# A list scheduler that keeps the port shared by GpSimd and VectorE as a resource, with all sums of activations on VectorE

## The chip, the cores and the metric

The kernel runs on one core of one Trainium2 chip. The metric is the device time of one execution in microseconds, as the median of the runs of a kernel; a profile of one further execution stands beside it.

## The reference

Three blocks are computed, all in float32. The attention block has 2 batches of 8 heads, 576 positions, 64 wide: a local attention (|i-j| < 4) plus an attention over means of 4 positions, repeated back up. Its output becomes x for two mixtures of experts:

```python
# MoE 1: N, D, E, F = 1152, 512, 8, 1024
P = np.exp(logits - logits.max())          # logits = x @ w_gate
for _ in range(8):                         # "gate rounds" below
    P /= P.sum(1, keepdims=True) + 1e-09
    P /= P.sum(0, keepdims=True) + 1e-09
    P *= N / E
for e in range(E):
    out += P[:, e:e + 1] * (np.maximum(x @ w1[e], 0.0) @ w2[e])
# MoE 2: the same with 4 experts; its P is given with the inputs
```

## The kernel before

All values are split into two parts, hi (rounded for TensorE) and lo (the rest), and each product runs as three passes (hi hi, hi lo, lo hi). A value `xh`, `xl` is such a pair. The first products `x @ w1` are not done block by block: as in Strassen's scheme, 7 products of sums of blocks take the place of 8, and a second level of the same scheme lies inside ("deep" products, line L507). So two kinds of sums are needed. **Sums of weights** (L355, and their lo parts at L328) are made anew for every expert, all on GpSimd (POOL in the profile). **Sums of activations** are made once for MoE 1 and once for MoE 2: `x_sums(j)`, four calls for four quarters of the tokens, adds hi and lo back to a whole value (L1129), combines four of those (L1135, into `tmp`), stores the combination (DMA to `kept`, L1145), and splits it again into `sh` (ScalarE, L1147) and `sl` (VectorE, L1149); `deep_sums(p, ...)` does the same for the second level of product p (L1209 for all its two-operand steps, L1228 for the hi part on ScalarE, into `sx`).

Before, these activation sums are dealt out between POOL and VectorE (DVE in the profile): L1129 is always on POOL, the rest by two tables.

```python
ON_POOL = (3, 5, 6, 7)              # L411: deep_sums of these products on POOL
X_POOL0, X_POOL = (1, 3), (0, 2)    # L1397: x_sums of these quarters on POOL, MoE 1 and MoE 2
```

The hidden layer leaves PSUM at L424 (ScalarE, relu, hi part) and L426 (VectorE, lo part): `own<-bank` where the source is in PSUM (a bank), `own<-tmp` where it was brought to SBUF before, so that L426 has two operands in SBUF. L482 adds banks, L527 copies a bank into another as the start of a product ("seed"; the product L507 then adds to it), L674 is the second product, L709 to L719 add its result to the output. At the start of MoE 2, `turn` (L1251 to L1263) brings MoE 1's output back as `xh`, `xl`. The gate of MoE 1 makes logits (L1279, copied out at L1286), transposes them (L1335, L1359), and does its eight rounds: row sums on VectorE (L1321 to L1325), column sums as a product with ones on TensorE (L1383), and L1386 to L1392 on VectorE.

The order on every engine is written out by `Plan`: each task is added with an engine, a cost in ns, what it reads and writes; `run` then takes, step by step, the task that can begin first by these costs, among the first 48 of each engine, and emits it. Queues are in order on the chip, so this order stays. There are two plans: one for attention and the first weights (up to about 71 us), a second one for all that follows.

Of the kernel before, what the change touches and what calls it, by code (L numbers as in the profile page):

```python
# [94 lines left out]
class Plan:  # L95
# [5 lines left out]
    QUEUE = 1  # L101
    PULL = 0.0
    OVER = dict.fromkeys(AFTER, 0.0)

    def __init__(self):
        self.tasks, self.last, self.readers = [], {}, {}
        self.clock, self.later, self.bias = 0.0, [], 0.0
        self.ranks, self.step = (), None

    def add(self, eng, cost, fn, reads=(), writes=(), slack=0.0, after=()):  # L110
        n = len(self.tasks)
        if self.step is not None:
# [22 lines left out]
        deps.discard(n)  # L135
        if eng == "PE":
            self.clock += cost
        self.tasks.append((eng, cost, fn, sorted(deps), bufs, self.clock + slack + self.bias))
        while self.later and self.clock >= self.later[0][0]:
            self.later.pop(0)[1]()  # L140

    def run(self, free=None, idle=None):
# [29 lines left out]
        for _ in range(len(T)):  # L172
            best = None
            for e in engines:
                look = self.QUEUE if e == "DMA" else self.LOOK
                mine = None
                for i in todo[e][:look]:
                    t = start(i)
                    if t is None:
                        continue  # L180

                    v = t + self.PULL * T[i][5]
                    if mine is None or v < mine[0] - 1e-9:
                        mine = (v, t, i)
# [5 lines left out]
            t, i, e = best  # L190
            if e == "PE":
                stall += t - free[e]
            _, cost, fn, _, bufs, _ = T[i]
            for b in bufs:
                if b.slot is not None:
                    continue
                since = b.ring.free()[0] + 150.0
                b.ring.give(b)
                if e == "PE" and idle is not None:
                    idle(b, t - max(free[e], since))  # L200
            if e == "DMA":
# [16 lines left out]
def tile_attention_moe_moe(  # L218
# [191 lines left out]
    SUMS = (0, 5, 2), (4, 3)  # L410
    ON_POOL = (3, 5, 6, 7)  # L411

# [7 lines left out]
    def hidden(src, key, s, b, u, c0, slack=0.0):  # L420
# [6 lines left out]
            out=ht[:, s, 1, c:c + U], in0=src(), scalar=0.0, in1=ht[:, s, 0, c:c + U].bitcast(F32),  # L427
            op0=ALU.max, op1=ALU.subtract), (key, (*k, 0)), ((*k, 1),), slack=slack)

    P_EVICT, S_EVICT = (412.0, 457.0), (420.0, 900.0)  # L430

# [676 lines left out]
    extra = [late.tile([128, U], F32, name=f"sum_{j}") for j in range(3)]  # L1108
    SHARED, PARTS = 900.0, 860.0
    SHARED_X, PARTS_X = 900.0, 900.0  # L1110
    LAG = 18000.0
# [3 lines left out]
    def x_sums(j, on_pool=False):  # L1115
# [21 lines left out]

# [5 lines left out]
        for i, t in enumerate((a22, a11, a21, a12)):  # L1143
# [58 lines left out]
    def deep_sums(p, g, on_pool):  # L1202
# [117 lines left out]
    def gate_rows():  # L1320
# [5 lines left out]
            out=pv, in0=pv, in1=sm_["rs"].unsqueeze(2).to_broadcast([128, NN, E1]), op=ALU.mult),  # L1326
            ("rs",), ("p",))

    def gate_start():
# [12 lines left out]
        def fill_eps():  # L1342
# [36 lines left out]
    def gate_round(it):  # L1379
        pc = r_bank.new()  # L1380
        def fn():
# [12 lines left out]
            in1=sm_["cs"].unsqueeze(1).to_broadcast([128, NN, E1]), op0=ALU.mult, op1=ALU.mult),  # L1394
            ("cs",), ("p", *done))
# [215 lines left out]
```

## Time and profile before

| what | value |
|---|---|
| median of 3 runs | 1176.58 us (1174.29 to 1176.61) |
| profiled execution, its time | 1174.57 us |
| its span in the profile | 1172.8 us |
| TensorE busy | 1151.8 us, 98% |
| VectorE busy | 845.7 us, 72% |
| GpSimd busy | 965.5 us, 82% |

The span runs from the first to the last instruction; the time of the same execution is 1.8 us more. Shares of busy time are averages over a span of very different stages: attention up to about 66 us, the gate and the first products of MoE 1 up to about 200, a long even stretch to 790, the passage to MoE 2 up to about 910, and an even stretch again.

### The profile page before, as it was taken

What the parts mean: (1) busy time and instruction counts of PE and PEld (TensorE: products, weight loads), DVE (VectorE), ACT (ScalarE), POOL (GpSimd) and SP (SyncE); (2) the same over time, 40 slices, a digit from 0 to 9 for tenths busy, and PEclk for the clock granted to TensorE, in tenths of its full rate; (3) what the DMA queues carried; (4) which work ended last, traced back from release to release, by engine and by line L of the source; (5) the groups of instructions that cost most, each with busy time, mean ns of one, the idle gap of its engine ahead of it and who ended that gap; (6) DMA issues with size and microseconds to landing.
All of it is one profiled execution on the core that took longest, in us unless ns stands there. A gap on an engine that the chain in (4) does not pass through costs nothing.

```text
span 1172.8 us, 22043 instructions
## 1 busy us (share of the span) xinstructions
PE 1151.8 (98%) x7361; PEld 1026.2 (87%) x7361; DVE 845.7 (72%) x1803; ACT 668.4 (57%) x1679; POOL 965.5 (82%) x1081
## 2 busy tenths in 40 slices
PE   9989899999999999999999999999799999999998
PEld 7868888988988988988988988989698898898897
DVE  7869789677668668568568568578788776766764
ACT  5844546755655655656556556535475565565561
POOL 7979958898798798798798798739999979879870
PEclk9999899999999999999999999999899999999999
DMA  8525344544544544544554654632535555555544
GB/s 247 161 96 169 131 136 145 181 164 158 184 159 158 180 166 152 184 168 146 188 171 138 195 167 139 207 113 82 177 123 166 175 179 163 164 173 164 161 159 144
DMA packets 110946, 188.66 MB, mean 161 GB/s; under 512 B 13360, under 2 KB 26416, under 8 KB 110832
## 3 DMA queue, kind: packets, MB, share of 16 engines
q1 hardware_dynamic: 110832, 187.25, 50.0%
q8 instruction: 58, 0.95, 0.3%
q14 instruction: 56, 0.46, 0.1%
HBM read 128.22 MB, written 58.98 MB: 160 GB/s over the span
## 4 chain that ended last, share of the span: by engine, by line
PE 85%; POOL 7%; DMA 3%; DVE 2%; issue 2%; ACT 1%; SPq 0%; POOLq 0%; DVEq 0%; ACTq 0%
PE bank L674 46%; PE bank L507 33%; PE bank L467 2%; POOL tmp L1129 1%; POOL raw L355 1%; PE bank L306 1%; POOL w2s L328 1%; POOL tmp L1135 1%; DMA v<-in_v_dram 1%; POOL own L328 1%; DVE sl L1149 1%; POOL sx L1209 1%; PE bank L1010 1%; DVE sx L1209 1%; PE bank L850 1%
## 5 line engine op out<-in xcount | busy, mean ns | idle before, releaser
L674 PE MATMUL bank<-w2s,own 128*128 128x512 f32 (+1 forms) x2604 | 671.4, 392 | 0.0
L674 PEld LDWEIGHTS bank<-w2s,own 128*128 128x128 f32 x2604 | 462.0, 188 | 69.5
L482 DVE TENSOR_TENSOR bank<-bank,tmp 128x288 f32<-128x288 f32 x540 | 221.7, 458 | 139.8 <-PE bank L507 64.6
L328 POOL TENSOR_TENSOR own<-raw,own 128x512 fp32r<-128x512 f32 (+1 forms) x204 | 244.0, 1205 | 56.0 <-ACT own L326 55.2
L355 POOL TENSOR_TENSOR raw<-raw,raw 128x128 f32<-128x128 f32 (+1 forms) x372 | 248.2, 677 | 13.6 <-DMA raw<-in_w1a_dram 1.8
L527 ACT ACTIVATE bank<-bank 128x288 f32<-128x288 f32 x426 | 169.6, 398 | 135.9 <-PE bank L507 132.6
L719 DVE SCALAR_TENSOR_TENSOR acc<-bank,prob,acc 128x512 f32<-128x512 f32 (+1 forms) x190 | 138.3, 742 | 110.5 <-DMA acc<-out_dram 74.4
L326 ACT ACTIVATE own<-raw 128x512 fp32r<-128x512 f32 (+1 forms) x204 | 114.5, 575 | 71.4 <-POOL raw L355 68.0
L320 ACT ACTIVATE tmp<-bank 128x288 f32<-128x288 f32 x230 | 90.5, 409 | 99.6 <-PE bank L507 62.0
L328 POOL TENSOR_TENSOR w1s_b<-raw,w1s_b 128x512 fp32r<-128x512 f32 (+1 forms) x100 | 119.5, 1199 | 29.3 <-ACT w1s_b L326 29.0
L482 DVE TENSOR_TENSOR tmp<-bank,tmp 128x288 f32<-128x288 f32 x344 | 138.9, 450 | 5.3 <-PE bank L507 3.9
L426 DVE SCALAR_TENSOR_TENSOR own<-bank,own 128x288 fp32r<-128x288 f32 x296 | 120.1, 448 | 22.1 <-ACT own L424 19.3
L328 POOL TENSOR_TENSOR w2s<-raw,w2s 128x512 fp32r<-128x512 f32 x96 | 126.1, 1323 | 8.0 <-ACT w2s L326 6.9
L355 POOL TENSOR_TENSOR raw<-raw 128x256 f32<-128x256 f32 x142 | 106.5, 756 | 31.1 <-PE bank L674 16.3
L507 PE MATMUL bank<-sx,own 128*128 128x288 f32 x687 | 118.4, 297 | 6.6 <-ACT bank L527 6.3
L424 ACT ACTIVATE own<-bank 128x288 fp32r<-128x288 f32 x296 | 108.3, 409 | 28.7 <-DVE bank L482 15.3
L507 PEld LDWEIGHTS bank<-sx,own 128*128 128x128 f32 x687 | 105.4, 190 | 16.0 <-ACT bank L527 8.1
L507 PE MATMUL bank<-xh,own 128*128 128x288 f32 x434 | 114.9, 294 | 0.0
L507 PE MATMUL bank<-sh,own 128*128 128x288 f32 x440 | 114.8, 294 | 0.0
L507 PEld LDWEIGHTS bank<-xh,own 128*128 128x128 f32 x434 | 79.6, 188 | 5.0
L507 PEld LDWEIGHTS bank<-sh,own 128*128 128x128 f32 x440 | 80.1, 188 | 3.8
L426 DVE SCALAR_TENSOR_TENSOR own<-tmp,own 128x288 fp32r<-128x288 f32 x88 | 77.9, 938 | 0.4 <-ACT own L424 0.4
(172 smaller groups left out, 1644.1 us busy)
## 6 DMA issues: line engine op xcount, KB each, us to landing
out_dram<-acc SPq DMA_DIRECT2D x206, 256.0 KB, 2.0
acc<-out_dram SPq DMA_DIRECT2D x198, 256.0 KB, 2.7
raw<-in_w1a_dram SPq DMA_DIRECT2D x94, 256.0 KB, 2.9
raw<-in_w2a_dram SPq DMA_DIRECT2D x64, 256.0 KB, 2.7
raw<-in_w1b_dram SPq DMA_DIRECT2D x46, 256.0 KB, 2.7
raw<-in_w2b_dram SPq DMA_DIRECT2D x32, 256.0 KB, 2.9
kept<-tmp SPq DMA_DIRECT2D x32, 144.0 KB, 2.1
qk<-in_qk_dram SPq DMA_DIRECT2D x7, 576.0 KB, 8.2
```

Of the source, the lines that this page charges most:

```text
L320: nc.scalar.activation(out=dst(), in_=src(), func=ACTF.Copy, **kw)
L326: plan.add("ACT", copy_cost(n), lambda: nc.scalar.activation(out=hi(), in_=src(), func=ACTF.Copy), keys, ((b, 0, 0),))
L328: plan.add("POOL", pool_cost(n), lambda: nc.gpsimd.tensor_tensor(out=lo(), in0=src(), in1=hi().bitcast(F32), op=ALU.subtract), (*keys, (b, ...
L355: plan.add("POOL", pool_cost(n), lambda: nc.gpsimd.tensor_tensor(out=out(), in0=x(), in1=y(), op=op), keys, (key,))
L424: plan.add("ACT", c0[0], lambda: nc.scalar.activation(out=ht[:, s, 0, c:c + U], in_=src(), func=ACTF.Relu), (key,), ((*k, 0),), slack=slack)
L426: plan.add("DVE", c0[1], lambda: nc.vector.scalar_tensor_tensor(out=ht[:, s, 1, c:c + U], in0=src(), scalar=0.0, in1=ht[:, s, 0, c:c + U]. ...
L467: nc.tensor.matmul(out=ps.slot[:, 0:U], lhsT=w.slot[:, j, k, 128 * (1 - q):128 * (1 - q) + 128], rhs=a[hl], start=(first and k == 0 and n ...
L482: plan.add("DVE", cost, lambda: nc.vector.tensor_tensor(out=get(dst), in0=get(ps), in1=get(b), op=ALU.add), tuple({ps, b} - {dst}), (dst,) ...
L507: nc.tensor.matmul(out=view(ps), lhsT=b.slot[:, j].rearrange("p k b -> p (k b)")[:, c:c + 128], rhs=place(a[hl]), start=(first and n == 0) ...
L527: nc.scalar.activation(out=view(dst), in_=view(src), func=ACTF.Copy)
L674: nc.tensor.matmul(out=ps.slot[:, 0:nd], lhsT=ht[:, j, a, 128 * n:128 * n + 128], rhs=w[j].slot[:, b, c0:c0 + nd], start=(j == 0 and p == ...
L719: plan.add("DVE", 130 + 1.2 * nd, lambda: nc.vector.scalar_tensor_tensor(out=a(), in0=ps.slot[:, 0:nd], scalar=prob[:, n, e:e + 1], in1=a( ...
```

## The change

The second plan keeps a time `port` up to which the port pair is taken. Tasks that read two operands from SBUF on VectorE (`both`), and all tasks on POOL, are put behind it; when choosing, the wait counts with a weight (`WAIT`), and POOL is allowed 200 ns (`GRACE`). Costs in the tables change. All activation sums go to VectorE.

```diff
+    WAIT = {"DVE": 0.5, "POOL": 1.0}
+    GRACE = {"DVE": 0.0, "POOL": 200.0}
...
+        if self.port is not None and (both or eng == "POOL"):
+            self.both.add(n)
...
-                    v = t + self.PULL * T[i][5]
+                    v, a = t + self.PULL * T[i][5], t
+                    if i in self.both:
+                        a = max(t + self.GRACE[e], self.port)
+                        v += self.WAIT[e] * (a - t - self.GRACE[e])
...
+                if i in self.both:
+                    end[i] = a + cost - self.GRACE[e]
+                    self.port = end[i] - (100.0 if e == "DVE" else 0.0)
...
-    ON_POOL = (3, 5, 6, 7)
+    ON_POOL = ()
...
-    P_EVICT, S_EVICT = (412.0, 457.0), (420.0, 900.0)
+    P_EVICT, S_EVICT = (412.0, 457.0), (435.0, 460.0)
...
     plan = Plan()
+    plan.port = 0.0
...
-    SHARED, PARTS = 900.0, 860.0
-    SHARED_X, PARTS_X = 900.0, 900.0
+    SHARED, PARTS = 420.0, 840.0
+    SHARED_X, PARTS_X = 420.0, 900.0
...
-                plan.add("POOL", PARTS_X, lambda t=t, o=o, h=h: nc.gpsimd.tensor_tensor(
+                plan.add("DVE", SHARED_X, lambda t=t, o=o, h=h: nc.vector.tensor_tensor(
...
-            sub(pool, full[i], lambda: h.bitcast(F32), lambda: l.bitcast(F32), part_keys(p, u), (keys[i],),
+            sub(pool if on_pool else dve, full[i], lambda: h.bitcast(F32), lambda: l.bitcast(F32), part_keys(p, u), (keys[i],),
...
-    X_POOL0, X_POOL = (1, 3), (0, 2)
+    X_POOL0, X_POOL = (), ()
```

The other changed lines mark the tasks of `both`: L426 where its source is in SBUF, the two-operand steps of `x_sums` and `deep_sums`, and four of the gate's. The change shifts line numbers in its file: L1129 becomes L1141, L1135 L1148, L1149 L1162, L1209 L1222, L1286 L1299, L1263 L1276, L328 L339, L355 L366, L426 L437.

On VectorE, at the start of the second plan, around the three copies of the gate's logits (`raw`), there stands before:

```order
L1135 TENSOR_TENSOR tmp_3_1339<-tmp_3_1339,tmp_2_1338 128x288
L1209 TENSOR_TENSOR sx_11_0_0_1323<-sx_12_0_0_1325,sx_11_0_0_1323 128x288
L1149 TENSOR_TENSOR sl_1300<-tmp_1_1337,sh_1299 128x2x144
L1286 COPY raw_0_85<-bank_0_89 16x384
L1149 TENSOR_TENSOR sl_1300<-tmp_2_1338,sh_1299 128x2x144
L1286 COPY raw_1_86<-bank_1_90 16x384
L1149 TENSOR_TENSOR sl_1300<-tmp_0_1336,sh_1299 128x2x144
L1286 COPY raw_2_87<-bank_2_91 16x384
```

and after the change:

```order
L1141 TENSOR_TENSOR tmp_0_1336<-xh_78,xl_79 128x288
L1141 TENSOR_TENSOR tmp_1_1337<-xh_78,xl_79 128x288
L1141 TENSOR_TENSOR tmp_2_1338<-xh_78,xl_79 128x288
L1141 TENSOR_TENSOR tmp_3_1339<-xh_78,xl_79 128x288
L1299 COPY raw_0_85<-bank_0_89 16x384
L1148 TENSOR_TENSOR tmp_1_1337<-tmp_0_1336,tmp_1_1337 128x288
L1141 TENSOR_TENSOR tmp_4_1340<-xh_78,xl_79 128x288
L1148 TENSOR_TENSOR tmp_0_1336<-tmp_2_1338,tmp_0_1336 128x288
L1299 COPY raw_1_86<-bank_1_90 16x384
L1148 TENSOR_TENSOR tmp_2_1338<-tmp_1_1337,tmp_2_1338 128x288
L1162 TENSOR_TENSOR sl_1300<-tmp_1_1337,sh_1299 128x2x144
L1299 COPY raw_2_87<-bank_2_91 16x384
```

The whole values `tmp<-xh,xl` have come over from POOL and stand ahead of the copies; a deep sum (`sx_11`) that stood ahead of the first copy and reads what POOL made has left the place. On POOL, at the same place of the program, before:

```order
L1345 MEMSET prob1_72 128x9
L1129 TENSOR_TENSOR tmp_0_1336<-xh_78,xl_79 128x288
L1129 TENSOR_TENSOR tmp_1_1337<-xh_78,xl_79 128x288
L1129 TENSOR_TENSOR tmp_2_1338<-xh_78,xl_79 128x288
L1129 TENSOR_TENSOR tmp_3_1339<-xh_78,xl_79 128x288
```

and after the change:

```order
L1358 MEMSET prob1_72 128x9
L339 TENSOR_TENSOR w1s_b_1296<-raw_3_88,w1s_b_1296 128x512
L339 TENSOR_TENSOR w1s_b_1296<-raw_4_1297,w1s_b_1296 128x512
L366 TENSOR_TENSOR raw_0_85<-raw_5_1298,raw_3_88 128x512
L366 TENSOR_TENSOR raw_2_87<-raw_1_86,raw_0_85 128x512
```

The activation sums are gone from POOL, and work on the weights follows at once. On VectorE, at the start of MoE 2, where `turn` makes `xl`, the order before is:

```order
L1263 TENSOR_TENSOR xl_79<-bank_4_93,xh_78 128x4x128
L1209 TENSOR_TENSOR sx_11_1_1_2338<-sx_5_0_2_8751,sx_11_0_1_2281 128x288
L426 SCALAR_TENSOR_TENSOR own_81<-bank_3_92,own_81 128x288
L1149 TENSOR_TENSOR sl_1300<-tmp_3_1339,sh_1299 128x2x144
L426 SCALAR_TENSOR_TENSOR own_81<-bank_1_90,own_81 128x288
L1149 TENSOR_TENSOR sl_1300<-tmp_7_1343,sh_1299 128x2x144
```

and after the change:

```order
L1276 TENSOR_TENSOR xl_79<-bank_5_94,xh_78 128x4x128
L1222 TENSOR_TENSOR sx_15_1_1_2715<-sx_8_1_2_8765,sx_15_0_1_2699 128x288
L437 SCALAR_TENSOR_TENSOR own_81<-bank_4_93,own_81 128x288
L1141 TENSOR_TENSOR tmp_3_1339<-xh_78,xl_79 128x288
L1141 TENSOR_TENSOR tmp_6_1342<-xh_78,xl_79 128x288
L1141 TENSOR_TENSOR tmp_5_1341<-xh_78,xl_79 128x288
L1276 TENSOR_TENSOR xl_79<-bank_3_92,xh_78 128x4x128
L1141 TENSOR_TENSOR tmp_8_1344<-xh_78,xl_79 128x288
```

Here too the whole values now stand among VectorE's own work, between the turned pieces and the lo parts of the hidden layer. TensorE's order hardly changes: 76 of some 4640 rows differ, nearly all of them neighbours that change places.

## Rows read from the trace of the kernel before

**Rows 1.** The page, part 1: busy us of each engine, share, instructions.
```profile
PE 1151.8 (98%) x7361; PEld 1026.2 (87%) x7361; DVE 845.7 (72%) x1803; ACT 668.4 (57%) x1679; POOL 965.5 (82%) x1081
```

**Rows 2.** Stretches: their length, busy PE, PEld, DVE, ACT, POOL (instructions), granted clock, DMA.
```profile
66.00:100.00 34.00, 29.83 (x216) 25.16 (x215) 26.01 (x49) 12.87 (x34) 29.83 (x33) 0.95 0.37 114
100.00:120.00 20.00, 19.20 (x93) 16.01 (x92) 16.65 (x24) 8.96 (x20) 19.26 (x17) 1.00 0.81 246
120.00:150.00 30.00, 26.23 (x168) 25.43 (x169) 23.05 (x58) 15.46 (x39) 27.75 (x31) 0.89 0.29 94
150.00:200.00 50.00, 50.00 (x288) 44.55 (x287) 43.93 (x102) 26.45 (x67) 31.64 (x35) 1.00 0.46 148
200.00:790.00 590.00, 590.00 (x3391) 527.83 (x3390) 413.18 (x887) 348.22 (x872) 487.71 (x554) 1.00 0.51 166
790.00:836.00 46.00, 46.00 (x295) 42.55 (x294) 38.04 (x60) 22.34 (x54) 43.80 (x45) 1.00 0.35 100
836.00:850.00 14.00, 7.66 (x34) 6.56 (x33) 7.71 (x9) 6.47 (x15) 14.00 (x16) 0.76 0.72 224
850.00:910.00 60.00, 59.15 (x342) 51.95 (x341) 48.83 (x95) 38.45 (x98) 57.75 (x63) 1.00 0.46 147
```

**Rows 3.** PE's timeline: start, us, instruction, and in brackets the idle time before.
```profile
84.42 0.35 PE L1335 MATMUL bank<-ident,raw 16*128 16x16 f32 x3 [2.55 <-DVE raw L1286]
...
120.69 0.43 PE L1383 MATMUL bank<-prob,ones 128*128 128x90 f32 x2 [1.49 <-DVE prob L1325]
...
135.01 0.73 PE L1383 MATMUL bank<-prob,ones 128*128 128x90 f32 x2 [3.09 <-DVE prob L1325]
...
843.54 1.09 PE L507 MATMUL bank<-sx,own 128*128 128x288 f32 x3 [6.34 <-ACT bank L527]
```

**Rows 4.** DVE's timeline at the first and third of these.
```profile
81.90 1.03 DVE L1209 TENSOR_TENSOR sx<-sx,sx 128x288 f32<-128x288 f32 x1 [4.53 <-POOL sx L1209]
...
130.70 1.06 DVE L1209 TENSOR_TENSOR sx<-sx,sx 128x288 fp32r<-128x288 f32 x1 [2.19 <-ACT sx L1228]
```

**Rows 5.** The chain that ended last in 836 to 844: start, us, what.
```profile
839.70 1.47 POOL own L328
841.17 0.97 POOL sx L1209
...
843.19 0.31 ACT bank L527
```

**Rows 6.** POOL's groups by form: busy us, mean ns of one, idle before.
```profile
L328 POOL TENSOR_TENSOR own<-raw,own 128x512 fp32r<-128x512 f32 x110 | 146.5, 1334 | 5.3 <-ACT own L326 5.2
L355 POOL TENSOR_TENSOR raw<-raw,raw 128x128 f32<-128x128 f32 x284 | 133.3, 478 | 9.1
...
L1129 POOL TENSOR_TENSOR tmp<-xh,xl 128x288 f32<-128x288 f32 x32 | 29.9, 957 | 7.4 <-ACT xh L1036 7.4
L1209 POOL TENSOR_TENSOR sx<-sx,sx 128x288 f32<-128x288 f32 x28 | 25.0, 905 | 0.0
L1135 POOL TENSOR_TENSOR tmp<-tmp,tmp 128x288 f32<-128x288 f32 x16 | 14.8, 923 | 0.0
```

**Rows 7.** DVE's groups by form: busy us, mean ns of one, idle before.
```profile
L719 DVE SCALAR_TENSOR_TENSOR acc<-bank,prob,acc 128x512 f32<-128x512 f32 x188 | 137.3, 744 | 108.9 <-DMA acc<-out_dram 74.4 <-PE bank L674 32.0 <-ACT acc L725 2.5
L426 DVE SCALAR_TENSOR_TENSOR own<-bank,own 128x288 fp32r<-128x288 f32 x296 | 120.1, 448 | 22.1 <-ACT own L424 19.3
L426 DVE SCALAR_TENSOR_TENSOR own<-tmp,own 128x288 fp32r<-128x288 f32 x88 | 77.9, 938 | 0.4 <-ACT own L424 0.4
```

**Rows 8.** DVE's timeline where POOL has ended, then POOL's at MoE 2.
```profile
160.19 0.45 DVE L1209 TENSOR_TENSOR sx<-sx,sx 128x288 fp32r<-128x288 f32 x1
160.55 0.20 DVE L1390 RECIPROCAL cs<-cs 128x8 f32<-128x8 f32 x1
...
791.20 3.11 POOL L1209 TENSOR_TENSOR sx<-xh,xl 128x288 f32<-128x288 f32 x4 [18.64 <-DVE xl L1263]
```

**Rows 9.** Line L1383, the column sums: min/median/max ns, first and last start.
```profile
L1383 PE MATMUL bank<-prob,ones x16: 238/274/518, 112.3 to 166.8; 128*128 128x90 f32 x16
```

More of the change, by code (lines that the diff above doesn't have):

```diff
@@ L108, in __init__, with add @@
         self.ranks, self.step = (), None
-    def add(self, eng, cost, fn, reads=(), writes=(), slack=0.0, after=()):
+        self.both, self.port = set(), None
+    def add(self, eng, cost, fn, reads=(), writes=(), slack=0.0, after=(), both=False):
         n = len(self.tasks)
+        if self.port is not None and (both or eng == "POOL"):
+            self.both.add(n)
         if self.step is not None:
@@ L180, in run @@
                         continue
-                    v = t + self.PULL * T[i][5]
+                    v, a = t + self.PULL * T[i][5], t
+                    if i in self.both:
+                        a = max(t + self.GRACE[e], self.port)
+                        v += self.WAIT[e] * (a - t - self.GRACE[e])
                     if mine is None or v < mine[0] - 1e-9:
-                        mine = (v, t, i)
+                        mine = (v, a, t, i)
                 if mine is not None and (best is None or mine[1] < best[0]):
@@ L189, in run @@
                 raise RuntimeError(f"nothing can begin: {[(T[i][0], T[i][3][-3:], [d for d in T[i][3] if not done[d]]) for i in left]}")
-            t, i, e = best
+            a, t, i, e = best
             if e == "PE":
@@ L427, in hidden @@
             out=ht[:, s, 1, c:c + U], in0=src(), scalar=0.0, in1=ht[:, s, 0, c:c + U].bitcast(F32),
-            op0=ALU.max, op1=ALU.subtract), (key, (*k, 0)), ((*k, 1),), slack=slack)
-    P_EVICT, S_EVICT = (412.0, 457.0), (420.0, 900.0)
+            op0=ALU.max, op1=ALU.subtract), (key, (*k, 0)), ((*k, 1),), slack=slack, both=c0 is S_EVICT)
+    P_EVICT, S_EVICT = (412.0, 457.0), (435.0, 460.0)
     def plain_unit(w, q, s, b, u, keys=None):
@@ L1128, in x_sums @@
                 t = part[b][h]
-                plan.add("POOL", PARTS_X, lambda t=t, o=o, h=h: nc.gpsimd.tensor_tensor(
+                plan.add("DVE", SHARED_X, lambda t=t, o=o, h=h: nc.vector.tensor_tensor(
                     out=v(t), in0=xh[:, 2 * h:2 * h + 2, o:o + wd].bitcast(F32),
-                    in1=xl[:, 2 * h:2 * h + 2, o:o + wd].bitcast(F32), op=ALU.add), [("x", n, h) for n in tiles], (t,))
+                    in1=xl[:, 2 * h:2 * h + 2, o:o + wd].bitcast(F32), op=ALU.add), [("x", n, h) for n in tiles], (t,),
+                    both=True)
         def two(dst, x, y, op):
@@ L1135, in two @@
             plan.add("POOL" if on_pool else "DVE", PARTS_X if on_pool else SHARED_X, lambda: e.tensor_tensor(
-                out=v(dst), in0=v(x), in1=v(y), op=op), (x, y), (dst,))
+                out=v(dst), in0=v(x), in1=v(y), op=op), (x, y), (dst,), both=True)
         (a21, a22), (a11, a12) = part
@@ L1150, in x_sums @@
                 out=lo, in0=v(t), in1=hi.bitcast(F32), op=ALU.subtract),
-                (t, ("s", i, j, 0)), (("s", i, j, 1),), after=own_keys("s", i))
+                (t, ("s", i, j, 0)), (("s", i, j, 1),), after=own_keys("s", i), both=True)
     sums, homes = {}, {}
@@ L1209, in sub @@
             plan.add(name, cost, lambda: e.tensor_tensor(
-                out=dst(), in0=x(), in1=y(), op=op), reads, writes, slack=LAG, after=after)
+                out=dst(), in0=x(), in1=y(), op=op), reads, writes, slack=LAG, after=after, both=True)
         def whole_part(i, u, k):
@@ L1310, in tile_attention_moe_moe, with gate @@
     sm_ = {}
-    def gate(eng, cost, fn, reads, writes):
+    def gate(eng, cost, fn, reads, writes, both=False):
         plan.add(eng, cost, fn, [("g", k) if isinstance(k, str) else k for k in reads],
-                 [("g", k) if isinstance(k, str) else k for k in writes], slack=FIRST)
+                 [("g", k) if isinstance(k, str) else k for k in writes], slack=FIRST, both=both)
     def small_tile(name, shape):
@@ L1326, in gate_rows @@
             out=pv, in0=pv, in1=sm_["rs"].unsqueeze(2).to_broadcast([128, NN, E1]), op=ALU.mult),
-            ("rs",), ("p",))
+            ("rs",), ("p",), True)
     def gate_start():
@@ L1350, in gate_start @@
         gate("DVE", 300.0, lambda: nc.vector.tensor_tensor(
-            out=pv, in0=lg2[:, :, 0:E1], in1=lg2[:, :, E1:], op=ALU.add), ("l",), ("p",))
+            out=pv, in0=lg2[:, :, 0:E1], in1=lg2[:, :, E1:], op=ALU.add), ("l",), ("p",), True)
         gate("DVE", 300.0, lambda: nc.vector.tensor_reduce(
@@ L1394, in gate_round @@
             in1=sm_["cs"].unsqueeze(1).to_broadcast([128, NN, E1]), op0=ALU.mult, op1=ALU.mult),
-            ("cs",), ("p", *done))
+            ("cs",), ("p", *done), True)
         if it < 7:
             gate_rows()
-    X_POOL0, X_POOL = (1, 3), (0, 2)
+    X_POOL0, X_POOL = (), ()
     first_w1 = [r_w1n.hold(b) for b in first_w1]
```

## The prediction

> **What bounds the kernel now.** I read the busy times first: TensorE works 1151.8 of 1172.8 us, so at most some 20 us are to be had unless its own work shrinks, and GpSimd, not VectorE, is the next fullest [rows 1]. Then the stretches, since a mean over the span hides where TensorE stands [rows 2]. From 150 to 836 TensorE is busy all the time at clock 1.00: there neither engine can give anything, only take. The lost time lies in two places. Between 66 and 150 TensorE is idle for 4.17 + 0.80 + 3.77 us (length less busy time), and the granted clock is 0.95 and 0.89 in the first and the third stretch, a mean of the two levels 1.2 and 2.4 GHz; on the busy time that costs 29.83 x 0.05 = 1.5 and 26.23 x 0.11 = 2.9. Between 836 and 850 it is idle for 6.34 us and runs at 0.76 (7.66 x 0.24 = 1.8), and to 910 another 0.85 is idle. So the clock falls behind each long stop, and a stop costs more than its own length.
>
> Third, what ended these stops [rows 3]: two waits on the gate (L1335 for VectorE's copies L1286, L1383 twice for L1325), and one, the longest, for ScalarE's copy of a bank (L527). A releaser is only the last link, so I followed each one back. At the first, VectorE stood 4.53 us for a deep sum on GpSimd before it came to the copies [rows 4]. At the third, VectorE's row sums stood behind a sum that waited 2.19 us for ScalarE's hi part [rows 4], whose input is a sum of GpSimd's. At the last, the chain is GpSimd through and through: a split of weights, a deep sum, then ScalarE's seed and TensorE [rows 5]. Three of the four stops so come from activation sums that wait in GpSimd's queue among weights; the second I take to be like the third.
>
> The ceiling by place: A (gate's copies) 4.2 + 1.5 = 5.7; B 0.8; C 3.8 + 2.9 = 6.7; D (MoE 2) 6.3 + 1.8 = 8.1; E (to 910) 0.85. Together 22.2 us.
>
> **The change part by part.** *What moves.* 104 instructions leave GpSimd; the three largest groups are 76 of them, at 0.91 to 0.96 us each [rows 6]. So GpSimd loses about 104 x 0.92 = 95 us, and all its weights come that much sooner in the stretches with the stops. On VectorE such an instruction takes 0.45 us alone, and the next one begins 0.36 after its start [rows 8]; next to a busy GpSimd it takes more. Of that, L426 gives a measure: 0.448 with one operand in SBUF, 0.938 with two [rows 7]. So 104 x 0.36 to 0.94 = 37 to 98 us come onto VectorE. In the even stretches nothing moves but neighbours, and TensorE's own order is the same but for neighbours and three short fills, under 0.5 us in all. The new costs and the port model change only orders, so I price them by the orders they give.
>
> *A.* Before the third copy L1286 stand 9 two-operand instructions, all on operands that VectorE or ScalarE have made; none waits for GpSimd any more. 9 x 0.45 us [rows 8] is 4 us, 8.5 at 0.94 [rows 7], against the 15.9 us from 66, where the second plan is about to begin, to 84.42 - 2.55 = 81.87, where TensorE comes to L1335 [rows 3]. That stop goes. What is late next is the chain behind it, transposes, copy, maximum, L1359, where the changed order puts two or three sums of 0.45 between links that TensorE covers with about 1.7 us of products: about 1.1 at L1359 and, with two sums again, 1.4 at the product behind it. I keep 2.6 for A (bounds 0, and 5.7 if all of it comes back). GpSimd's weights hide behind the wait for their loads there.
>
> *B and C.* The row sums are now behind sums on VectorE alone and not behind a link VectorE - GpSimd - ScalarE - VectorE. But VectorE carries all the sums of four quarters, 48 two-operand instructions where it had 24. The column sums come (166.8 - 112.3) / 7 = 7.8 us apart on average [rows 9], 7.1 without the two stops of 1.49 and 3.09 [rows 3]. In the changed order the fullest round has 13 two-operand instructions ahead of its row sums, and the gate's own six small ones, as L1390 or a little longer (0.20 to 0.45 [rows 8]), are 1.2 to 2.7: 7.1 to 8.6 us alone, 13.4 to 14.9 with 13 x 0.94 next to a GpSimd that never stops. I take 1.0 for all the rounds together, since the mean of VectorE before is 23.05 of 30 us there [rows 2]; bounds 0 and 9 (14.9 - 7.1 = 7.8 for the fullest, a little for the next). In 150 to 200 VectorE was already 43.93 of 50 us full [rows 2], and 6 more sums of 0.45 come: 46.6 of 50. I take 1.0 (0 to 4).
>
> *D.* This is the largest term and the one most in doubt. In the changed order 92 instructions of VectorE stand from the first sum of MoE 2 to the last that the seed L527 needs: 68 with two operands in SBUF, 16 like L426 from a bank, 8 of 512 columns like L719. Alone that is 68 x 0.36 to 0.45, 16 x 0.36 to 0.45 and 8 x 0.744 [rows 7, 8]: 36.2 to 43.8 us. There is room from 791.20, when the first inputs are there [rows 8], to 843.54 - 6.34 = 837.20, when TensorE stops [rows 3], less 1.4 us from a sum's end (841.17 + 0.97) to TensorE's start [rows 5, 3]: 44.6 us. So alone VectorE comes 1 to 8 us early. GpSimd has 24 weight instructions in that time, of 0.478 to 1.334 us [rows 6], 11 to 32 us, the middle of which is 22. If every one of VectorE's sums beside them takes 0.938 and not 0.45, 22 us hold 23 of them, and the rest is 45 x 0.36 to 0.45: 22 + 16 to 20 + 12 to 13 = 50 to 55 us, 5 to 10 late. But GpSimd had 18.64 us idle ahead of 791.20 [rows 8], in which it now can make weights, held up by loads and buffers only, and the order puts sums where GpSimd waits. I take 2.0 (bounds 0 and 10).
>
> How much one holds up the other shows in rows: a sum on GpSimd takes 0.957 on average [rows 6] against 3.11 / 4 = 0.78 with little beside it [rows 8], and L426 loses 0.49 us [rows 7]. That is part of an instruction, not a whole one of 1.334. The Trainium skill, "SBUF — State Buffer", section "Who interferes with whom", speaks against this change: a VectorE instruction with two SBUF inputs contends with a GpSimd instruction that reads SBUF, the shared pair is an exclusive lock, and the one that comes second fully blocks. By that rule each weight instruction of GpSimd would stop VectorE for its length; the rows' averages, with either one first, don't decide it.
>
> *E.* 15 sums go from GpSimd to VectorE between 850 and 910, where it was 48.83 of 60 us busy [rows 2]: 48.8 + 15 x 0.45 = 55.6. I keep 0.5 of 0.85 (0 to 3).
>
> *Sum.* What stays: 2.6 + 1.0 + 1.0 + 2.0 + 0.5 = 7.1 us of new or old stops. Gain 22.2 - 7.1 = 15.1, so the profiled execution of 1174.57 becomes 1159.5. The median of the runs lies 2.0 above that execution, the lowest run 0.3 below; I add 0.5: **1160.0**.
>
> **Rivals.**
> - *The port is VectorE's new queue (slower).* Each weight instruction beside D stops VectorE for its whole length: 11 to 32 us on top of 36.2 to 43.8, with the middle of each 62 against 44.6, so TensorE stops 17 us at D; by the same measure the fullest gate rounds lose up to 9 and 150 to 200 its 4. 2.6 + 9 + 4 + 17 + 3 = 36 against 22 before: 1174.6 + 14 = 1188. It decides from 24.5 us of stops on: with rounds, 150 to 200 and E at these bounds when D's instructions take over 44.6 + 5.9 = 50.5 us, with the others as I take them only at 64. For it: VectorE's 0.938 [rows 7]; against it: that this is half a us, not 1.3. By the Trainium skill, "SBUF — State Buffer", section "Who interferes with whom", it would go this way wherever GpSimd is first. Chance 0.08.
> - *The stops only change their owner.* GpSimd is early, VectorE as late as GpSimd was: with D at 10, A at 5, rounds at 4, E at 1, 20 us stay: 1174.57 - 2.2 + 0.5 = 1173, and with 6 less 1167. For it: VectorE is 88% busy at 150 to 200 [rows 2], and it has no idle engine to hand work to. Against it: at A its wait of 4.53 was for GpSimd, not for itself [rows 4]. Chance 0.18, of which 0.10 ends within 0.2% of before.
> - *All stops go.* The planner's order fits and nothing is late: 1174.57 - 22.2 + 0.5 = 1152.9 (1152 to 1155). For it: alone, VectorE is early everywhere. Chance 0.12.
>
> **How the numbers follow.** My forecast, most stops gone and a rest of 3 to 13 us (1155 to 1166), has 0.62. 0.2% of the time (2.3 us) is about what a measurement of this kernel can tell from no change. Faster: 0.62 + 0.12 + 0.08 = 0.82; same: 0.10; slower: 0.08. The range runs from 1153, all stops gone, to 1172, where the second rival still gains; it leaves out the slower rival and the no-change part, 0.18 in all, and a little below. The likeliest case has 1155 to 1166 for itself.
>
> **What the profile after would show.** GpSimd's busy time falls by about 95 us to some 870 or a little less, as its weights meet other neighbours; VectorE's rises to between 880 and 940. TensorE's busy time, which holds its slow stretches, falls a few us, its idle time from 21 to about 10. Right at A: no wait at L1348 for the copies, short ones at L1372 and L1383 (in the changed lines). Right at D: the product behind the seed waits under 4 us, and its chain back goes through VectorE. Wrong, if TensorE waits there over 8 us for ScalarE or VectorE behind a row of sums of about 0.9 us each; if the column sums of the rounds (L1396) wait for the row sums in more than two rounds; or if the even stretch from 200 to 790 shows idle TensorE, since then the new cost of L426 with two operands, set to that of one, has put it where a bank is needed.

## The result and the profile after

| | before | after |
|---|---|---|
| median | 1175.43 us (4 runs, 1173.29 to 1176.61) | 1163.98 us (4 runs, 1162.33 to 1165.08) |
| profiled execution, span | 1174.57, 1172.8 us | 1165.08, 1163.2 us |

The ratio is 0.9903, with a 95% interval of 0.9883 to 0.9924: 11.4 us less, where 16.6 were forecast, inside the stated range. Busy times first (the page, part 1; compare [rows 1]):

```profile
PE 1148.7 (99%) x7362; PEld 1023.4 (88%) x7362; DVE 854.5 (73%) x1907; ACT 673.8 (58%) x1679; POOL 872.5 (75%) x977
```

GpSimd gave up 93 us for 104 instructions; VectorE took the same 104 and grew by 9 only. The stretches, with the columns of [rows 2]; where the program now runs earlier the borders are moved by 5 to 10 us:

```profile
66.00:100.00 34.00, 33.56 (x250) 28.40 (x249) 26.09 (x65) 14.98 (x36) 10.89 (x8) 1.00 0.32 106
100.00:120.00 20.00, 20.00 (x111) 17.61 (x110) 19.32 (x44) 12.99 (x30) 10.13 (x8) 1.00 0.88 269
120.00:150.00 30.00, 29.71 (x187) 27.14 (x186) 29.01 (x79) 12.00 (x30) 19.37 (x22) 1.00 0.43 140
150.00:200.00 50.00, 49.19 (x283) 43.53 (x282) 49.39 (x110) 30.59 (x76) 31.62 (x33) 1.00 0.46 149
200.00:780.00 580.00, 579.17 (x3336) 518.83 (x3335) 396.37 (x876) 348.17 (x864) 476.34 (x545) 1.00 0.51 166
780.00:830.00 50.00, 47.98 (x306) 44.19 (x305) 47.88 (x87) 22.21 (x54) 22.77 (x21) 1.00 0.36 101
830.00:845.00 15.00, 11.75 (x56) 9.72 (x55) 14.00 (x33) 10.62 (x27) 5.70 (x7) 0.89 0.71 215
845.00:905.00 60.00, 59.18 (x353) 53.23 (x352) 53.04 (x106) 36.18 (x92) 46.89 (x48) 1.00 0.52 163
```

TensorE's idle time (length less busy) is 0.44 + 0 + 0.29 up to 150, where it was 4.17 + 0.80 + 3.77, and the clock there is 1.00 throughout. Between 780 and 845 it is 2.02 + 3.25, where 6.34 stood. TensorE's timeline has the stops that are left (columns as in [rows 3]):

```profile
129.13 0.46 PE L1396 MATMUL bank<-prob,ones 128*128 128x90 f32 x2 [0.29 <-DVE prob L1338]
...
796.68 0.66 PE L1264 MATMUL bank<-ident,acc 128*128 128x128 f32 x4 [2.02 <-DVE acc L730]
...
834.81 0.67 PE L518 MATMUL bank<-sx,own 128*128 128x288 f32 x3 [2.88 <-ACT bank L538]
```

The second of these is new: `turn` waits for VectorE's last addition to the output. VectorE's timeline ahead of it, and GpSimd's, show why:

```profile
788.70 1.54 DVE L1222 TENSOR_TENSOR sx<-sx,sx 128x288 f32<-128x288 f32 x1
790.16 1.53 DVE L1222 TENSOR_TENSOR sx<-xh,xl 128x288 f32<-128x288 f32 x1
791.62 0.74 DVE L730 SCALAR_TENSOR_TENSOR acc<-bank,prob,acc 128x512 f32<-128x512 f32 x1
792.28 2.35 DVE L1222 TENSOR_TENSOR sx<-sx,sx 128x288 f32<-128x288 f32 x2
...
797.15 0.44 DVE L1222 TENSOR_TENSOR sx<-sx,sx 128x288 fp32r<-128x288 f32 x1
```

```profile
788.40 5.92 POOL L339 TENSOR_TENSOR w2s<-raw,w2s 128x512 fp32r<-128x512 f32 x4 [22.91 <-DMA acc<-out_dram]
...
810.01 0.74 POOL L366 TENSOR_TENSOR raw<-raw 128x256 f32<-128x256 f32 x1 [15.69 <-DMA raw<-in_w1b_dram]
```

While GpSimd splits four blocks, a sum on VectorE comes at 788.70 and the next at 790.16, 1.46 us apart; a few us later, with GpSimd idle, one takes 0.44. The four splits take 5.92 / 4 = 1.48 us each, so GpSimd pays too. They stand there after a wait of 22.91 us, which the trace puts down to a DMA.

One correction to the sum of stops. The first plan is the same program, but its end differs from execution to execution; the logits' products begin (line rows of L1279, before, and of L1292, after):

```profile
L1279 PE MATMUL bank<-xh,wg_a x12: 331/338/338, 76.0 to 79.8; 128*16 128x384 f32 x12
```

```profile
L1292 PE MATMUL bank<-xh,wg_a x12: 332/338/339, 78.4 to 82.3; 128*16 128x384 f32 x12
```

So the profiled execution after came to the logits 2.4 us late; instruction for instruction of TensorE, this lateness is there in full by 32 us, in attention. From there to the end it took 1163.2 - 78.4 = 1084.8 against 1172.8 - 76.0 = 1096.8: 12.0 us less from the logits on.

### The profile page after: what moved, and what is told of

The parts are those of the page before. It is cut to its first block, busy times and chain, and to the rows that moved or that the text cites. A ratio compares the mean times of both kernels' runs of the same rounds, so it can differ in the third digit from the quotient of the medians.

```text
span 1163.2 us, 22042 instructions
## 1 busy us (share of the span) xinstructions
PE 1148.7 (99%) x7362; PEld 1023.4 (88%) x7362; DVE 854.5 (73%) x1907; ACT 673.8 (58%) x1679; POOL 872.5 (75%) x977
## 4 chain that ended last, share of the span: by engine, by line
PE 87%; DVE 9%; DMA 2%; issue 1%; ACT 0%; POOL 0%; SPq 0%; POOLq 0%; DVEq 0%
PE bank L685 47%; PE bank L518 33%; DVE sx L1222 2%; PE bank L317 2%; PE bank L478 2%; DMA v<-in_v_dram 1%; DVE own L437 1%; DVE sl L1162 1%; DVE tmp L1148 1%; DVE tmp L1141 1%; PE bank L763 1%; DVE xl L1222 0%; PE bank L1021 0%; DVE bank L493 0%; DVE acc L730 0%
## 5 line engine op out<-in xcount | busy, mean ns | idle before, releaser
L493 DVE TENSOR_TENSOR bank<-bank,tmp 128x288 f32<-128x288 f32 x540 | 225.8, 459 | 141.1 <-PE bank L518 77.9
L339 POOL TENSOR_TENSOR own<-raw,own 128x512 fp32r<-128x512 f32 (+1 forms) x204 | 241.2, 1194 | 71.8 <-ACT own L337 70.1
L366 POOL TENSOR_TENSOR raw<-raw,raw 128x128 f32<-128x128 f32 (+1 forms) x372 | 249.6, 684 | 20.0 <-DMA raw<-in_w1b_dram 6.8
L730 DVE SCALAR_TENSOR_TENSOR acc<-bank,prob,acc 128x512 f32<-128x512 f32 (+1 forms) x190 | 140.6, 741 | 111.9 <-DMA acc<-out_dram 65.1
L339 POOL TENSOR_TENSOR w1s_b<-raw,w1s_b 128x512 fp32r<-128x512 f32 (+1 forms) x100 | 119.6, 1203 | 73.6 <-ACT w1s_b L337 68.1
L339 POOL TENSOR_TENSOR w2s<-raw,w2s 128x512 fp32r<-128x512 f32 x96 | 125.5, 1318 | 41.3 <-DMA acc<-out_dram 22.9
L435 ACT ACTIVATE own<-bank 128x288 fp32r<-128x288 f32 x296 | 113.5, 410 | 47.6 <-DVE bank L493 39.7
L366 POOL TENSOR_TENSOR raw<-raw 128x256 f32<-128x256 f32 x142 | 106.1, 754 | 45.8 <-PE bank L685 21.8
L437 DVE SCALAR_TENSOR_TENSOR own<-bank,own 128x288 fp32r<-128x288 f32 x296 | 120.7, 446 | 15.3 <-ACT own L435 13.8
L518 PE MATMUL bank<-sx,own 128*128 128x288 f32 x687 | 119.1, 297 | 4.6 <-ACT bank L538 3.8
L518 PEld LDWEIGHTS bank<-sx,own 128*128 128x128 f32 x687 | 105.0, 190 | 14.7 <-ACT bank L538 5.8
L518 PE MATMUL bank<-xh,own 128*128 128x288 f32 x434 | 115.0, 294 | 0.0
L518 PE MATMUL bank<-sh,own 128*128 128x288 f32 x440 | 114.7, 294 | 0.0
L518 PEld LDWEIGHTS bank<-xh,own 128*128 128x128 f32 x434 | 79.8, 188 | 4.9
L518 PEld LDWEIGHTS bank<-sh,own 128*128 128x128 f32 x440 | 80.1, 189 | 3.7
L518 PE MATMUL bank<-sl,own 128*128 128x288 f32 x220 | 64.7, 294 | 0.0
```

The lines of the kernel that those rows point to most:

```text
L339: plan.add("POOL", pool_cost(n), lambda: nc.gpsimd.tensor_tensor(out=lo(), in0=src(), in1=hi().bitcast(F32), op=ALU.subtract), (*keys, (b, ...
L366: plan.add("POOL", pool_cost(n), lambda: nc.gpsimd.tensor_tensor(out=out(), in0=x(), in1=y(), op=op), keys, (key,))
L435: plan.add("ACT", c0[0], lambda: nc.scalar.activation(out=ht[:, s, 0, c:c + U], in_=src(), func=ACTF.Relu), (key,), ((*k, 0),), slack=slack)
L437: plan.add("DVE", c0[1], lambda: nc.vector.scalar_tensor_tensor(out=ht[:, s, 1, c:c + U], in0=src(), scalar=0.0, in1=ht[:, s, 0, c:c + U]. ...
L493: plan.add("DVE", cost, lambda: nc.vector.tensor_tensor(out=get(dst), in0=get(ps), in1=get(b), op=ALU.add), tuple({ps, b} - {dst}), (dst,) ...
L518: nc.tensor.matmul(out=view(ps), lhsT=b.slot[:, j].rearrange("p k b -> p (k b)")[:, c:c + 128], rhs=place(a[hl]), start=(first and n == 0) ...
```

## The experiments

The first question was whether taking the sums out of GpSimd's queue is enough (theory A, that of the prediction), or whether the order that the port model gives is what pays (rival B). Three kernels take the change apart. `move_only`:

```diff
-    plan.port = 0.0
...
-    P_EVICT, S_EVICT = (412.0, 457.0), (435.0, 460.0)
+    P_EVICT, S_EVICT = (412.0, 457.0), (420.0, 900.0)
...
-    SHARED, PARTS = 420.0, 840.0
-    SHARED_X, PARTS_X = 420.0, 900.0
+    SHARED, PARTS = 900.0, 860.0
+    SHARED_X, PARTS_X = 900.0, 900.0
```

> The changed kernel with its activation sums on VectorE, but with the planner as before: no port, and the old costs (900 ns for a two-operand instruction of VectorE). Theory A (the gain comes from taking the activation sums out of GpSimd's queue, whatever the model): 1162 to 1168, within 4 us of the changed kernel, GpSimd's busy time again about 872 us. Rival B (the order that the port model gives is what pays): 1172 or more, with VectorE's L437 of two SBUF operands back at about 0.94 us and new stops where sums stand beside weights.

`move_costs`, from the changed kernel:

```diff
-    plan.port = 0.0
```

> The changed kernel with its new costs (420 ns for a sum, 460 for L437) and the sums on VectorE, but no port in the planner. Theory A: 1162 to 1167, as the changed kernel. Rival B: slower than the changed kernel by 5 us or more, since the planner now packs sums beside weights without knowing that they hold each other up.

`model_only`, from the changed kernel (L1141 goes back to GpSimd too):

```diff
-    ON_POOL = ()
+    ON_POOL = (3, 5, 6, 7)
...
-            sub(pool if on_pool else dve, full[i], lambda: h.bitcast(F32), lambda: l.bitcast(F32), part_keys(p, u), (keys[i],),
+            sub(pool, full[i], lambda: h.bitcast(F32), lambda: l.bitcast(F32), part_keys(p, u), (keys[i],),
...
-    X_POOL0, X_POOL = (), ()
+    X_POOL0, X_POOL = (1, 3), (0, 2)
```

> The port model and the new costs, but the activation sums dealt out to GpSimd and VectorE as before. Theory A: no gain, 1172 to 1180, with the stops at the gate's copies, the column sums and the seed of MoE 2 as before. Rival B: 1162 to 1168 with GpSimd's busy time still about 960 us.

| kernel | median us | before, same chip | ratio, 95% interval |
|---|---|---|---|
| move_only | 1213.53 | 1176.66 | 1.0314 (1.0298 to 1.0329) |
| move_costs | 1188.35 | 1176.66 | 1.0104 (1.0089 to 1.0118) |
| model_only | 1180.55 | 1176.66 | 1.0032 (1.0020 to 1.0043) |

Both theories fall in their pure form: theory A at the first two, rival B at the third. Every part alone is slower than before, only the two together are faster. (The port in the planner without the new costs was not run.) The waits of TensorE (what it waited for, us in total, times, longest) are long single stops. In `move_only`, of those for L518:

```profile
PE bank L518 <- ACT sx L1240: 22.2, 4, 12.3
PE bank L518 <- DVE sx L1221: 13.0, 4, 10.1
```

and in `move_costs`:

```profile
PE bank L518 <- ACT bank L538: 12.4, 5, 10.2
PE bank L1395 <- DVE prob L1337: 11.1, 3, 6.6
```

The stop of 10.2 is that of MoE 2's seed. VectorE's timeline there, and GpSimd's:

```profile
846.32 7.22 DVE L1221 TENSOR_TENSOR sx<-sx,sx 128x288 f32<-128x288 f32 x7
853.46 0.45 DVE L1221 TENSOR_TENSOR xl<-sx,xh 128x288 fp32r<-128x288 f32 x1
```

```profile
845.94 1.61 POOL L339 TENSOR_TENSOR own<-raw,own 128x512 fp32r<-128x512 f32 x1
847.52 1.49 POOL L339 TENSOR_TENSOR w1s_b<-raw,w1s_b 128x512 fp32r<-128x512 f32 x1
848.97 2.10 POOL L366 TENSOR_TENSOR raw<-raw,raw 128x128 f32<-128x128 f32 x2
```

Seven sums that the plan counted at 420 ns each take 1.02 us each beside GpSimd's weights, so what was written as early comes late. In `move_only`, with 900 counted for each, VectorE's rows before the stop of 12.3 mostly follow 0.37 us apart: I read that as sums that the plan, too dear, put too late, not as collisions. Before its second stop (10.1 us, up to 861.1) there are collisions: from 843.75 to 856 VectorE's sums stand beside GpSimd's weights, and six of them take 1.48 to 1.55 us each. In `model_only` the longest stop is GpSimd's queue again (the chain that ended last in 882 to 907, a piece of it):

```profile
891.01 2.26 POOL own L339 x2
893.27 0.41 POOL raw L366
893.68 0.75 POOL sx L1222
894.43 1.86 POOL raw L366 x2
...
897.18 0.76 POOL sx L1222
```

`port_probe` measures the disputed price by itself.

```diff
...
+    def dve_two():
+        nc.vector.tensor_tensor(out=xo, in0=xa, in1=xb, op=ALU.add)
+    def dve_one():
+        nc.vector.tensor_tensor(out=xo, in0=bank[:, 0:288], in1=xb, op=ALU.add)
+    def pool_split():
+        nc.gpsimd.tensor_tensor(out=wo, in0=wa, in1=wb, op=ALU.subtract)
...
```

> No part of the reference is computed: VectorE and GpSimd run instructions of the kernel's sizes alone and side by side, and zeros are written out. Theory S (they share, as the means of the rows before suggested): beside splits of 128x512 on GpSimd a two-operand instruction of 288 columns on VectorE takes some 0.9 us and the split stays under 1.5. Theory L (whole-instruction lock): each of the two waits for the other's whole instruction, so that both come at one period of about 0.4 + 1.1 = 1.5 us, and a VectorE instruction with one operand in PSUM stays at 0.45 beside the same splits.

Its timeline, VectorE and GpSimd together; L267 is a split of 512 columns on GpSimd, L261 a sum with two operands in SBUF, L264 one with an operand in PSUM, both of 288 columns:

```profile
10.97 4.38 DVE L264 TENSOR_TENSOR xo<-bank,xb 128x288 f32<-128x288 f32 x9
...
11.20 10.66 POOL L267 TENSOR_TENSOR wo<-wa,wb 128x512 fp32r<-128x512 f32 x8
...
31.42 11.31 POOL L267 TENSOR_TENSOR wo<-wa,wb 128x512 fp32r<-128x512 f32 x8
31.56 11.97 DVE L261 TENSOR_TENSOR xo<-xa,xb 128x288 f32<-128x288 f32 x9
...
104.00 0.46 DVE L264 TENSOR_TENSOR xo<-bank,xb 128x288 f32<-128x288 f32 x1
104.49 0.91 DVE L261 TENSOR_TENSOR xo<-xa,xb 128x288 f32<-128x288 f32 x1
105.44 0.46 DVE L264 TENSOR_TENSOR xo<-bank,xb 128x288 f32<-128x288 f32 x1
105.93 0.91 DVE L261 TENSOR_TENSOR xo<-xa,xb 128x288 f32<-128x288 f32 x1
```

Theory L holds for VectorE. With an operand in PSUM, 4.38 / 9 = 0.49 us and the split 10.66 / 8 = 1.33: neither minds the other. With both in SBUF, the sums come at (11.97 - 0.49) / 8 = 1.43 us, one for each split, and the splits at 11.31 / 8 = 1.41. So VectorE waits for a whole split, and GpSimd loses 0.08 us.

The 0.94 us of L426 in the kernel before is then no price of one collision, but a mean of different waits. The timelines of VectorE and GpSimd there, in narrow windows, show single rows:

```profile
240.86 1.24 POOL L328 TENSOR_TENSOR own<-raw,own 128x384 fp32r<-128x384 f32 x1
241.15 1.27 DVE L426 SCALAR_TENSOR_TENSOR own<-tmp,own 128x288 fp32r<-128x288 f32 x1
...
282.92 0.56 POOL L355 TENSOR_TENSOR raw<-raw,raw 128x128 f32<-128x128 f32 x1
283.08 0.71 DVE L426 SCALAR_TENSOR_TENSOR own<-tmp,own 128x288 fp32r<-128x288 f32 x1
...
283.72 0.44 DVE L426 SCALAR_TENSOR_TENSOR own<-tmp,own 128x288 fp32r<-128x288 f32 x1
283.72 1.60 POOL L328 TENSOR_TENSOR w1s_b<-raw,w1s_b 128x512 fp32r<-128x512 f32 x1 [0.24 <-ACT w1s_b L326]
284.09 1.54 DVE L426 SCALAR_TENSOR_TENSOR own<-tmp,own 128x288 fp32r<-128x288 f32 x1
```

Each of the three long rows ends 0.31 or 0.32 us behind the end of GpSimd's row: 241.15 + 1.27 = 242.42 behind 242.10, 283.79 behind 283.48, 285.63 behind 285.32. The whole trace agrees: 19 of the 88 take about 0.45, and each of the other 69 ends 0.31 to 0.32 us behind the end of an instruction of GpSimd. So VectorE waits for the rest of whatever GpSimd is doing: 33 of the 88 take 0.7 to 0.9 us, 20 take over 1.4.

The next four keep the sums on VectorE and change only what the planner believes.

```diff
# flat640
-    plan.port = 0.0
-    SHARED, PARTS = 420.0, 840.0
-    SHARED_X, PARTS_X = 420.0, 900.0
+    SHARED, PARTS = 640.0, 840.0
+    SHARED_X, PARTS_X = 640.0, 900.0
-    P_EVICT, S_EVICT = (412.0, 457.0), (435.0, 460.0)
+    P_EVICT, S_EVICT = (412.0, 457.0), (435.0, 750.0)
# wait0
-    WAIT = {"DVE": 0.5, "POOL": 1.0}
+    WAIT = {"DVE": 0.0, "POOL": 0.0}
# grace0, grace300 (and below grace230, grace185 in the same way)
-    GRACE = {"DVE": 0.0, "POOL": 200.0}
+    GRACE = {"DVE": 0.0, "POOL": 0.0}
+    GRACE = {"DVE": 0.0, "POOL": 300.0}
```

> Sums on VectorE, no port in the planner, but flat costs near what the profile of the changed kernel shows on average beside GpSimd: 640 ns for a sum and 750 for L437 with two SBUF operands (in place of 420 and 460, or 900 and 900). Theory C (the written order pays only when its costs come true on the chip; a cost that depends on who else is running can be met on average by a flat one): 1164 to 1172. Theory D (the port must be known to the planner, since an instruction costs 0.45 or 1.45 and never 0.64): 1176 or more, with stops where several sums stand beside splits.

> The changed kernel with the weights of the wait at 0 for both engines: the planner still counts that one holds up the other, but no longer prefers tasks that need not wait. Theory C: about as the changed kernel, 1162 to 1168, since the times stay true. Rival E (avoiding the collisions is what pays): 1170 or more, with L437's mean back from 0.75 towards 0.94 us.

> The changed kernel with GpSimd's grace at 0 in place of 200 ns: each of its instructions is counted as longer by some 0.2 us where it meets VectorE. The probe showed a split with a sum beside it at 1.41 to 1.44 us against 1.33 alone, so a cost without grace is too high by about 0.2 us. Theory C: slower than the changed kernel, 1168 to 1180, since GpSimd is planned as full and the order puts weights first. If the exact number does not matter: 1162 to 1168.

> The changed kernel with GpSimd's grace at 300 in place of 200 ns, nearer to what the probe showed (a sum of 0.46 beside a split adds 0.1 us to the split, so some 0.36 of the sum is hidden). Theory C: as fast as the changed kernel or faster by 1 to 3 us: 1160 to 1165.

The last four ask where the gain is made, and how much of it is the chance of one order. In `moe1_moved` the sums of MoE 1 are on VectorE and those of MoE 2 dealt out as before, in `moe2_moved` the reverse; `grace230` and `grace185` change one number of the model by 30 and 15 ns.

```diff
# moe1_moved (moe2_moved: g < E1, and (1, 3), () below)
+    OLD = lambda g: g >= E1
...
+                work.append(lambda p=p: deep_sums(p, g, OLD(g) and p in (3, 5, 6, 7)))
...
+    X_POOL0, X_POOL = (), (0, 2)
```

> The changed kernel (port, new costs) with the sums of MoE 1 on VectorE, those of MoE 2 dealt out to GpSimd and VectorE as before. Theory M (each place gains by its own move): the stops up to 210 us stay as small as in the changed kernel, the one at the start of MoE 2 comes back with 8 to 15 us: 1168 to 1178. Rival O (one order is better than another by chance, and the place does not matter): any time from 1162 to 1180, with the stops at other places than these.

> The mirror image: the sums of MoE 2 on VectorE, those of MoE 1 as before. Theory M: stops of 8 to 15 us between 66 and 210, and from 780 to 910 the 8 to 10 us of lost time of the changed kernel: 1168 to 1178. Rival O: as above.

> The changed kernel with GpSimd's grace at 230 in place of 200 ns, a change of 30 ns that means nothing on the chip, but shifts the written order. If the model makes the gain whatever the order's details: 1161 to 1168. If the order's details matter as much as the model (Rival O): off by 5 us or more, as grace 300 was with 1170.

> The same with 185 ns. If the model makes the gain whatever the order's details: 1161 to 1168. Rival O: off by 5 us or more.

Idle is TensorE's, length less busy time in the rows of the stretches, from 66 to 210 and from 780 to 950.

| kernel | median us | ratio, 95% interval | idle 66 to 210 | idle 780 to 950 |
|---|---|---|---|---|
| before | 1174.8 to 1176.7 | 1 | 8.74 | 7.19 |
| changed kernel | 1163.98 | 0.9903 (0.9883 to 0.9924) | 2.38 | 6.09 |
| flat640 | 1177.77 | 1.0021 (1.0011 to 1.0031) | 7.50 | 9.25 |
| wait0 | 1172.70 | 0.9977 (0.9963 to 0.9991) | 6.35 | 7.39 |
| grace0 | 1178.63 | 1.0029 (1.0017 to 1.0041) | 9.95 | 8.59 |
| grace300 | 1170.05 | 0.9956 (0.9944 to 0.9969) | 4.78 | 6.30 |
| moe1_moved | 1174.27 | 1.0002 (0.9990 to 1.0014) | 3.17 | 16.49 |
| moe2_moved | 1170.96 | 0.9968 (0.9959 to 0.9978) | 6.85 | 8.46 |
| grace230 | 1164.51 | 0.9917 (0.9898 to 0.9936) | 1.15 | 7.34 |
| grace185 | 1169.21 | 0.9955 (0.9941 to 0.9969) | 4.93 | 8.38 |

- `flat640`: theory C's guess that a flat mean would do is wrong, theory D's 1176 or more is right. Its two prices, 0.45 or 1.45, are not all there is, as the rows above show, but a plan with one price for every wait is wrong nearly each time (2 of those 88 lie between 0.5 and 0.7).
- `wait0`: rival E's numbers came, 1172.7 us and L437 with two SBUF operands back at 0.918 (0.750 after): counting the wait is not enough, the order must also avoid it. Of the 88 rows of L437, 41 take under 0.5 us after the change and 2 over 1.4; in `wait0` it is 22 and 21, near the 19 and 20 of before. It is still under before, by 2 us.
- `grace0`, `grace300`: too much port time loses all of the gain, as expected; the value nearer to the probe was expected to be as good or better and lost 6 us.
- `moe1_moved`, `moe2_moved`: both times in the expected range, with the stops at the expected ends; that of `moe2_moved` is 6.1 us, where 8 to 15 were expected. TensorE's timelines of `model_only` (the first two rows), `moe2_moved` and `moe1_moved` have the same two stops:

```profile
166.94 0.61 PE L518 MATMUL bank<-sx,own 128*128 128x288 f32 x1 [6.19 <-ACT sx L1241]
906.35 0.61 PE L518 MATMUL bank<-sx,own 128*128 128x288 f32 x1 [12.97 <-ACT sx L1241]
...
164.62 0.61 PE L519 MATMUL bank<-sx,own 128*128 128x288 f32 x1 [6.13 <-ACT sx L1243]
...
905.01 0.61 PE L519 MATMUL bank<-sx,own 128*128 128x288 f32 x1 [13.83 <-ACT sx L1243]
```

So each move takes away the stop of its own place and leaves the other. These are not the stops of the kernel before, though: with the port in the planner and the old dealing they end at 167 and 906 us, where the old ones ended at 84 to 135 and at 843.5. By the ratios to before, against `model_only`, the move of MoE 1's sums is worth 0.0030, that of MoE 2's 0.0064, and both together 0.0129: some 3.5, 7.5 and 15 us. Against the kernel before, MoE 1's move with the new planner gains nothing (1.0002).

- `grace230`, `grace185`: one the same as the changed kernel, one 5 us slower. So the details of an order are worth some 5 us for changes that mean nothing on the chip. All four settings of the grace from 185 to 300 are faster than before, and all three kernels with the sums on VectorE and no port (costs 420, 640 and 900) are slower. (The profiled executions behind the idle times lie up to 3 us from the medians.)

No kernel here beats the changed one; `grace230` can't be told from it.

## Why the prediction was right, and where it was not

**The direction and the place: right.** The stops at the gate, the column sums and the seed went or shrank, as its steps said, and the parts from `moe1_moved` and `moe2_moved` lie at those two places.

**The terms.** Ceiling 22.2; measured rest, as idle time by stretch: A 0.4, nearly all of it a stop of attention before the gate (forecast 2.6), B and C 0.3 (1.0), 150 to 200 0.8 and just behind it 0.8 (1.0), D 2.0 + 3.25 idle and 11.75 x 0.11 = 1.3 of clock (2.0), E 0.8 (0.5). Together 9.7 in place of 7.1, a gain of 12.5 against 12.0 measured from the logits on. So D was mis-sized, 6.6 for 2.0, and A over-priced by 2.2. In D the term left out one place: the wait of `turn` for VectorE's L730, 2.02 us, behind sums that four splits held up. The rest between 12.0 and the 9.5 of the two profiled executions is the start, which came 2.4 us later. TensorE's idle time over the whole span fell from 21 to 14.5 us, not to about 10. One sign of being wrong came, but small: the even stretch from 200 shows 0.83 us of idle time, all before 203 us and for sums and a seed, not for L426.

**"That is part of an instruction, not a whole one": wrong.** The prediction read the mean of 0.94 as the price of one collision and set the rule of the Trainium skill, "SBUF — State Buffer", section "Who interferes with whom", aside as undecided. The probe has 1.43 us for a sum beside a split of 1.33, and the kernel 1.46: the one that comes second blocks until the first is through, as that page says. For VectorE as the second the rows show it in full; for GpSimd they show less, 0.08 us in the probe and 1.60 in place of some 1.33 us beside the row of 0.44 at 283.72. A mean over a form hides waits of every length; rows of single ones, next to GpSimd's, were in the trace of the kernel before and would have told.

**"37 to 98 us come onto VectorE": wrong.** It was 8.8. The moved instructions are not added to a fixed load: with GpSimd's sums gone and the rest ordered around the port, what stood on VectorE before got cheaper. VectorE's groups by form after, and the one of before that answers to the second (for the first compare the 0.938 of [rows 7]):

```profile
L437 DVE SCALAR_TENSOR_TENSOR own<-tmp,own 128x288 fp32r<-128x288 f32 x88 | 64.3, 750 | 0.0
L1162 DVE TENSOR_TENSOR sl<-tmp,sh 128x288 fp32r<-128x288 f32 x32 | 17.2, 558 | 0.0
...
L1149 DVE TENSOR_TENSOR sl<-tmp,sh 128x288 fp32r<-128x288 f32 x32 | 25.6, 823 | 3.7 <-ACT sh L1147 3.7
```

**The cause it named was half of it.** Its reasons were about queues: sums wait in GpSimd's. That is true, since `model_only` gains nothing and the chain of its longest stop runs mostly through that queue. But by these reasons `move_only` and `move_costs` should have gained as well, and they lost 37 and 12 us. The rival "the port is VectorE's new queue" names what happens there, at least in `move_costs`, whose sums take 1.02 us beside weights. The change escapes it because its order counts 0.42 for a sum alone and a wait where a weight is in the way, and puts the sum where it need not wait: with the wait counted but not avoided (`wait0`), 2 of the 11 us are left. The prediction had this in its hands only as "I price them by the orders they give". That the time fell inside its range is in part luck: a grace of 185 in place of 200 ns, of which none of its steps speaks, gives 1169.2, and no weight on the wait 1172.7, beyond the end of the range.

**Open.** How much of the last 5 us is the model's merit and how much the luck of one order can't be told from single kernels: 185, 200, 230 and 300 ns gave 1169.2, 1164.0, 1164.5 and 1170.1. It is not the start: from the logits to the end their profiled executions take 1092.7, 1084.8, 1085.4 and 1089.8 us. Why attention ends up to 5 us apart (logits from 75.4 to 80.3 us over the profiles) is open.

## What to carry to other kernels

Work moved from one engine to another that shares a port with it pays only if the order is written with the price that it has beside its new neighbours, and steers round it; a flat mean price does not do, because a collision here cost whatever was left of the other engine's instruction, from nothing to all of it. Look at single rows, not at a form's mean, before pricing contention: when the long ones all end the same short time behind an end on the other engine, it is a lock. And when the order comes from a list scheduler, try a few settings that mean nothing to learn how much of a gain is the order's luck; here it was 5 of 11 us.

## What the runs showed of the hardware that was not expected

- The lock is lopsided. Beside back-to-back splits of 512 columns, a two-operand sum of 288 columns on VectorE goes from 0.49 to 1.43 us, the split from 1.33 to 1.41. In the kernel before, a split that begins together with such an instruction pays more: the one at 283.72 takes 1.60, where the mean of its form with `own` is 1.334 [rows 6].
- What VectorE waits for is the rest of the running instruction of GpSimd: all 69 long rows of L426 end 0.31 to 0.32 us behind an end on GpSimd.
- An instruction of VectorE with an operand in PSUM fits into that wait for nothing: alternating the two kinds beside the splits, a pair takes 105.93 - 104.49 = 1.44 us, the same as a sum by itself beside them.
